# A half block's PSUM banks, the last row scatters, and the place of one expert's weight sums in a fused attention and mixture-of-experts kernel

## Chip, cores and metric

The kernel runs on one core of a Trainium2 chip. The metric is the device time of one execution in microseconds (us); lower is better. The engines are TensorE (PE, with its weight loads PEld), VectorE (DVE), ScalarE (ACT), GpSimd (POOL) and SyncE (SP, which here issues most DMAs).

## The reference

A gated linear attention is followed by a router and eight experts. Everything is float32.

```python
# q, k, v, alpha: (4, 8, 768, 48)
for t in range(S):
    state = alpha[:, :, t, :, None] * state + k[:, :, t] (outer) v[:, :, t]
    y[:, :, t] = q[:, :, t] @ state
x = y.transpose(0, 2, 1, 3).reshape(3072, 384)
...
logits = normalised(x) @ normalised(expert_emb).T / tau      # 8 experts
expert = argmax(logits); gate = softmax(logits)[expert]
out[rows of e] = gate * (relu(x[rows of e] @ w1[e]) @ w2[e])  # w1 384x1024, w2 1024x384
```

A token goes to one expert only, so its row of the output is one scaled product of that expert's two layers.

## The kernel before, in words

**Attention and routing.** The 3072 tokens are 24 chunks of 128 (NS = 24). A loop over s runs NS + 3 turns as a software pipeline: a chunk's decays are made in turn s, its scores in s + 1, its state and output in s + 2, its row of logits (`rows`) behind that. `scores` (L559) makes the products of keys and queries in two halves; the first half is masked by DVE (L571), the second is copied by ACT (L572) and masked by POOL with an `affine_select` (L573). From time to time a group of chunks is routed: `place` counts where each token belongs, and `to_rows` (L312) scatters the rows of a chunk with an indirect DMA issued by POOL (L313) to `xs`, a buffer in DRAM sorted by expert. Chunks wait for this in the list `send`. In turn s < NS one or two chunks are sent; from s = NS on all that are left. `behind(s)` puts an instruction after the last ones of turn s; `tc.issue_after` does the same with one named instruction. Both set only the order on an engine and the place in the program.

**Experts.** They are taken in an order found at run time, each with its turn i from 0 to 7. `xs` is read back in blocks of 128 rows (`xg`). PE transposes a block (`pxg`, L837), DVE or ACT copies it to `xT` (L841). The first layer gives `hT`, the second `y`, which POOL scatters to the rows of `out` (L812). Turn 0 is the leading expert: two of its blocks were read early and their first layer (`phe`, `ehT`) and second layer (L901, scaled by DVE at L904, columns `esx`) are done among the last routing work. Then it has one plain block (`first_layer` L889 and L893, `second_layer` L895 to L906). Turns 1 to 7 are *pairs*: three blocks. In the first layer all three go through Strassen-like products: `first_layer_pair` (L976) multiplies sums of `w1` and `xT`, each over 192 columns of tokens, into four PSUM banks `pq0` to `pq3` (matmuls L994, DVE sums through `by_dve` L917, ACT L1002 and L1005). In the second layer block 2 is plain, and blocks 0 and 1 go through `second_layer_pair` (L1027, matmuls L1042, DVE L1049).

Three kinds of sums feed these products:

- `mix_weights` (L931): eight POOL subtractions over `w2` of one expert into `w_m` (L941, some 1 us each). `turn_of(done_pair)` places them behind what is in `done_pair`: the last product, the last DVE operation and the last scatter of the pair before. For expert 1 there is no such pair, so `done_pair` is at first the list `routed`, that is the counts of the routing and the first two scatters of pad rows.
- `mix_hidden` (L943): DVE sums of `hT` into `hT_m`, for two `f` at a time, placed by `filled` (L920) among the next first-layer products.
- `mix_first` (L971): DVE sums for the next expert's first layer.

**Half blocks.** An expert can have more rows than its full blocks hold. `run_extra` (L1148) loads the number of such half blocks of 64 rows, behind `done_pair`, and enters a run-time If (L1151, L1155). Inside, `half_block` (L1074) has two groups of 48 small matmuls (L1084; 96 in the profile's counts), each group into one bank that `bank()` hands out of `pq0` to `pq3`, with a relu by ACT (L1089). Then come 32 in the second layer (L1097), DVE scales one half of the result (L1102) and ACT the other (L1103), and a POOL scatter follows (L812). On this data the If is taken in turns 0, 3 and 4. After turn 3 `run_rest` (L1168) tests once whether any expert has more.

**PSUM.** Pool `ps_q` has the banks `pq0` to `pq3`, one buffer each; `ps_y` has the bank `pyo`, two buffers in turn, for the plain second layer. The scheduler places instructions by these dependences, and a product of the next expert goes ahead of the If where the banks and order allow it.

The functions that the diff touches follow.

Of the kernel before, what the change touches and what calls it, by code (L numbers as in the profile page):

```python
# [9 lines left out]
FP32 = mybir.dt.float32  # L10
# [17 lines left out]
def kernel(  # L28
# [12 lines left out]
    nc = tc.nc  # L41
    B, H, S, D = q.shape
    E, DM = expert_emb.shape
    F = w1.shape[2]
    P = 128
# [4 lines left out]
    NS = N // P  # L50
# [149 lines left out]
    with ExitStack() as c1:  # L200
# [258 lines left out]
        def behind(s):  # L459

            queue = ExitStack()
            for call in st[s]["last"]:
                queue.enter_context(tc.issue_after(call.ins))
            return queue
# [94 lines left out]
        def scores(s):  # L559

            d = st[s]
            kr, qs = d["kr"], d["qs"]
            d["sm"] = sm = [work.tile([P, NP, P], FP32, name=f"sm{hh}") for hh in range(2)]
            sc = [ps_sc.tile([P, NP, P], FP32, name=f"sc{hh}") for hh in range(2)]
            for p in range(NP):
                for hh in range(2):
                    sl = slice(DP * hh, DP * hh + DP)
                    mm(
                        sc[hh][:, p], lhsT=kr[sl, p], rhs=qs[sl, p], start=True, stop=True
                    )  # L570
            nc.vector.tensor_tensor(sm[0], sc[0], causal.to_broadcast([P, NP, P]), ALU.mult)  # L571
            nc.scalar.copy(sm[1], sc[1])  # L572
            nc.gpsimd.affine_select(  # L573
                out=sm[1], in_=sm[1], pattern=[[0, NP], [1, P]], base=0,
                channel_multiplier=-1, compare_op=ALU.is_ge, fill=0.0,
            )
# [106 lines left out]
        for s in range(NS + 3):  # L683
            if s + 2 <= NS:
                v_last = load(s + 2)
            if s + 2 == NS:

                with tc.issue_after(v_last.ins):
                    weights(0)
            if 0 <= s - 1 < NS:  # L690
                with in_turn():
                    keys_back(s - 1)
            if s < NS:
                decays(s)
            if s == NS:
                with in_turn():
                    turn_early()
            if s < NS:
                decay_queries(s)
            if 0 <= s - 1 < NS:  # L700
                decay_state(s - 1)

                with in_turn(), tc.issue_after(st[s]["a_scan"].ins) if s < NS else ExitStack():
                    scores(s - 1)
            if s == 0:
                with behind(s), in_turn():
                    prepare_first(a0)
                with behind(s):
                    prepare_logits()
            if NS <= s < NS + 2:  # L710
                with in_turn():
                    first_layer_early(2 * (s - NS), 2 * (s - NS) + 1)
            if 0 <= s - 2 < NS:
                with in_turn():
                    mix_states(s - 2)
                with in_turn():
                    mix_chunk(s - 2)
            if 0 <= s - 1 < NS:

                with in_turn(), tc.issue_after(st[s]["a_scan"].ins) if s < NS else ExitStack():  # L720
                    update(s - 1)
            if 0 < s < NS and s % NCH == 0:

                with in_turn():
                    keys_back(s, ps_mm, "mm")
            if NS <= s < NS + 2:
                with in_turn():
                    first_layer_early(2 * (s - NS) + 1, 2 * (s - NS) + 2)
            if 0 <= s - 2 < NS:
                with in_turn():  # L730
                    rows(s - 2)
            if s == 1:
                with in_turn():
                    turn_logits()
            if s == 2:
                with behind(s):
                    routing_constants()
            if s == 3:
                with behind(s):
                    convert_constants()  # L740
            if 4 <= s < 4 + NXG * (NC + 1):
                i, t = divmod(s - 4, NC + 1)
                with behind(s):
                    nc.gpsimd.memset(xg_s[i][:, t], 0.0)
            if s == 3:
                with behind(s):
                    nc.gpsimd.memset(blank, 0.0)

            for g in placed_at.get(s, ()):
                r = GROUPS[g][1] - 1  # L750
                with in_turn():
                    n = place(g, r in (S0 - 1, NS - 1))
                if r == S0 - 1:
                    with behind(s):
                        first_expert(n)
            with behind(s) if s < NS else ExitStack():
                for c in send[:] if s >= NS else send[: 1 + (len(send) > 2)]:
                    to_rows(dest[:, c : c + 1], x_g[group_of[c]][:, c - GROUPS[group_of[c]][0]])
                    send.remove(c)
                    if c == S0 - 1:  # L760
                        fetch_early()
            if s == NS - 1:
                weights(1)
            r = s - 2
            if 0 <= r < NS:
                g = group_of[r]
                if r == GROUPS[g][1] - 1:
                    choose(g)
                    with behind(s) if s < NS else ExitStack():
                        nc.gpsimd.tensor_copy(x_g[g][:, :, TK], toks[:, slice(*GROUPS[g])])  # L770
            if s > NS:
                with in_turn():
                    first_layer_early(2 * (s - NS) + 2, 2 * (s - NS) + 4)
# [6 lines left out]
    with ExitStack() as c3:  # L780
# [24 lines left out]
        def bank(j=None):  # L805
            if j is None:
                taken.append(0)
                j = len(taken) % 4
            return ps_q.tile([P, 512], FP32, name=f"pq{j}")
# [85 lines left out]
        def second_layer(w2_t, hT, gate, col):  # L895

            py = ps_y.tile([P, DM], FP32, name="pyo")
            y = yp.tile([P, DM], FP32, name="y")
            with pe_turn():
                for f in range(FT):  # L900
                    pe[:] = [nc.tensor.matmul(  # L901
                        py, lhsT=hT[:, f], rhs=w2_t[:, f], start=(f == 0), stop=(f == FT - 1),
                    )]
            nc.vector.tensor_scalar(y, py, gate, None, ALU.mult)  # L904
            with turn_of(drained):
                return scatter(y, col)  # L906
# [167 lines left out]
        def half_block(w1_t, w2_t, xT, gate, col):  # L1074

            hT = hp.tile([P, FT, HALF], FP32, name="hT_half", bufs=1)
            for f0 in range(0, FT, 4):
                ph = bank()[:, 0 : 4 * HALF]

                for f in range(4):  # L1080
                    for k in range(KT):
                        for i in range(2):
                            c0 = (f0 + f) * P + i * HALF
                            nc.tensor.matmul(  # L1084
                                ph[i * HALF : (i + 1) * HALF, f * HALF : (f + 1) * HALF],
                                lhsT=w1_t[:, k, c0 : c0 + HALF], rhs=xT[:, k],
                                start=(k == 0), stop=(k == KT - 1), skip_group_check=True,
                            )
                nc.scalar.activation(  # L1089
                    hT[:, f0 : f0 + 4].rearrange("p f t -> p (f t)"), ph, AF.Relu  # L1090
                )

            py = ps_y.tile([P, DM], FP32, name="pyo")[:, 0 : DM // 2]
            y = yp.tile([P, DM], FP32, name="y")
            for f in range(FT):
                for i in range(2):
                    nc.tensor.matmul(  # L1097
                        py[i * HALF : (i + 1) * HALF], lhsT=hT[:, f],
                        rhs=w2_t[:, f, i * DM // 2 : (i + 1) * DM // 2],
                        start=(f == 0), stop=(f == FT - 1), skip_group_check=True,  # L1100
                    )
            nc.vector.tensor_scalar(y[0:HALF, 0 : DM // 2], py[0:HALF], gate, None, ALU.mult)  # L1102
            nc.scalar.mul(y[0:HALF, DM // 2 :], py[HALF:], gate)  # L1103
            scatter(y[0:HALF], col)

        def run(i):
# [32 lines left out]
                    drained.append(nc.gpsimd.drain())  # L1139
            gate, col = gt_s[i % NG], sx_s[i % NG]  # L1140
            for t in range(2 if pair else 0, blocks_run(i)):
                second_layer(
                    w2_t, hT[:, :, t * P : (t + 1) * P], gate[:, t : t + 1], col[:, t : t + 1]
                )
            if pair:
                second_layer_pair(w2_t, hT, gate, col)

# [109 lines left out]
```

## Time and profile before

| what | value |
|---|---|
| median of 3 runs | 427.87 us (427.85 to 428.65) |
| profiled execution, its own time | 429.66 us |
| its span | 427.9 us |
| instructions in the span | 10636 |
| granted clock of TensorE, mean | 1.00 |
| PE busy | 412.1 us (96%) |
| VectorE busy | 276.6 us (65%) |
| ScalarE busy | 177.3 us (41%) |
| GpSimd busy | 191.7 us (45%) |

The profile shows one execution. The span runs from the first to the last instruction; the execution's own time has 1.8 us more. A timeline row has the start (from the span's start) and the duration in us, the engine, the line of the code, the operation with its tiles, how often it ran in a row, and in brackets the idle time of that engine ahead of it and what ended it. The last routing work lies from about 144 to 163 us, the early blocks and the first layer of turn 0 from 163.6 to 182.6, turn 0's plain second layer and half block from 182.6 to 193.5. After that a pair starts at about every 31 us, and the ones behind a half block 6 us later.

### The profile page before, as it was taken

How to read it: one execution, taken by the hardware profiler on the slowest of the kernel's cores; microseconds unless marked ns; L12 is line 12 of the kernel's file. 1: busy time of each engine (PE TensorE's matmuls, PEld its weight loads, DVE VectorE, ACT ScalarE, POOL GpSimd, SP SyncE). 2: the span in 40 equal slices, each digit the busy share in tenths (PEclk: the TensorE clock that was granted, in tenths of full speed). 3: DMA queues.
4: the chain of work that ended last, by engine and by line, in shares of the span. 5: the costliest groups of instructions: out<-in, count | busy, mean ns of one | idle time of the engine just before them, and what ended most of it. 6: DMA issues, size and time to landing. Idle time of an engine off the chain costs nothing. (4 is left out here: it accounts for less than half of the span.)

```text
span 427.9 us, 10636 instructions
## 1 busy us (share of the span) xinstructions
PE 412.1 (96%) x3962; PEld 363.6 (85%) x3962; DVE 276.6 (65%) x725; ACT 177.3 (41%) x430; POOL 191.7 (45%) x283
## 2 busy tenths in 40 slices
PE   7999999999999999999999999999999999998995
PEld 6988889888898876779799799798888979978984
DVE  6888778788798424945856846823781684683631
ACT  4455454554455435363623523522361352352410
POOL 6455776677865628801018027024501802702601
PEclk9999999999999999999999999999999999999999
DMA  8999899999979903859009119016502801001001
GB/s 138 158 155 165 145 205 184 195 184 201 197 170 333 351 36 120 276 196 373 6 17 343 57 46 361 5 54 209 163 20 89 303 2 36 20 1 52 1 17 38
DMA packets 119371, 60.15 MB, mean 141 GB/s; under 512 B 102287, under 2 KB 113816, under 8 KB 119312
## 3 DMA queue, kind: packets, MB, share of 16 engines
q1 hardware_dynamic: 115208, 49.14, 49.2%
q0 software_dynamic: 3728, 10.16, 6.7%
q8 instruction: 38, 0.62, 0.7%
q14 instruction: 21, 0.17, 0.1%
q10 hardware_dynamic: 376, 0.05, 0.1%
HBM read 49.69 MB, written 11.45 MB: 143 GB/s over the span
## 5 line engine op out<-in xcount | busy, mean ns | idle before, releaser
L812 POOL DMA_INDIRECT out_dram<-y,sx x25 | 24.5, 979 | 164.5 <-DVE xT_m L971 81.1
L994 PE MATMUL pq<-xT,w 128*128 128x192 f32 x280 | 64.3, 328 | 1.0 <-PEq L1155 0.6
L994 PEld LDWEIGHTS pq<-xT,w 128*128 128x128 f32 x280 | 47.4, 190 | 2.5 <-issue 2.5
L917 DVE TENSOR_TENSOR hT<-pq,v 128x192 f32<-128x192 f32 x84 | 29.9, 356 | 27.9 <-PE pq L994 25.6
L507 POOL TENSOR_TENSOR qs<-qc,a 128x512 f32<-128x512 f32 x24 | 30.7, 1278 | 37.0 <-DVE a L503 22.6
L901 PE MATMUL pyo<-w,hT 128*128 128x384 f32 x128 | 43.3, 492 | 0.0
L994 PE MATMUL pq<-xT_m,w_m 128*128 128x192 f32 x168 | 36.8, 328 | 2.7 <-ACTq L1155 1.2
L901 PEld LDWEIGHTS pyo<-w,hT 128*128 128x128 f32 x128 | 23.7, 190 | 15.3
L1002 ACT ACTIVATE hT<-hT 128x384 f32<-128x384 f32 (+1 forms) x56 | 24.7, 443 | 24.4 <-DVE hT L917 19.5
L479 DVE TENSOR_TENSOR_SCAN r<-pa,inr 128x511 f32<-128x511 f32 x24 | 29.2, 1218 | 7.6 <-PE pa L194 7.1
L994 PEld LDWEIGHTS pq<-xT_m,w_m 128*128 128x128 f32 x168 | 28.7, 190 | 3.7 <-ACTq L1155 1.8
L503 DVE TENSOR_TENSOR_SCAN a<-pa,ini 128x512 f32<-128x512 f32 x24 | 29.3, 1223 | 1.1
L1042 PE MATMUL pq<-w_m,hT_m 128*128 128x192 f32 x168 | 29.6, 326 | 0.0
L941 POOL TENSOR_TENSOR w_m<-w 128x384 f32<-128x384 f32 x28 | 27.6, 1005 | 4.0 <-DMA out_dram<-y,sx 1.7
L1002 ACT ACTIVATE hT<-pq 128x192 f32<-128x192 f32 x28 | 9.3, 331 | 47.3 <-PE pq L994 47.3
L917 DVE TENSOR_TENSOR v<-pq,v 128x192 f32<-128x192 f32 x56 | 20.0, 357 | 13.7 <-PE pq L994 6.0
L191 PE MATMUL sc<-qs,kr 64*128 64x128 f32 x384 | 28.6, 290 | 0.0
L313 POOL DMA_INDIRECT xs<-x,dest x24 | 24.4, 1016 | 9.4 <-issue 4.5
L1042 PEld LDWEIGHTS pq<-w_m,hT_m 128*128 128x128 f32 x168 | 27.7, 190 | 0.0
L191 PEld LDWEIGHTS sc<-qs,kr 64*128 64x128 f32 x384 | 24.1, 193 | 4.2 <-issue 3.0
L941 POOL TENSOR_TENSOR w_m<-w,w_m 128x384 f32<-128x384 f32 x28 | 27.0, 998 | 0.0
L191 PE MATMUL pyx<-sm,vt 128*64 128x128 f32 x384 | 26.3, 279 | 0.0
(199 smaller groups left out, 896.1 us busy)
## 6 DMA issues: line engine op xcount, KB each, us to landing
w<-in_moe_w_dram SPq DMA_DIRECT2D x16, 1536.0 KB
kt<-in_k_dram SPq DMA_DIRECT2D x24, 192.0 KB
qt<-in_q_dram SPq DMA_DIRECT2D x24, 192.0 KB
vt<-in_v_dram SPq DMA_DIRECT2D x24, 192.0 KB
xg<-xs SPq DMA_DIRECT2D x22, 196.5 KB
at<-in_alpha_dram SPq DMA_DIRECT2D x24, 168.0 KB
xg<-xs SPq DMA_DIRECT2D x8, 98.2 KB
at<-in_alpha_dram SPq DMA_DIRECT2D x24, 22.5 KB
```

The lines of the kernel that those rows point to most:

```text
L191: last["pe"] = nc.tensor.matmul(*args, **kwargs)
L313: ins = nc.gpsimd.indirect_dma_start(out=xs, out_offset=bass.IndirectOffsetOnAxis(ap=rows, axis=0), in_=x, in_offset=None, bounds_check=E ...
L479: nc.vector.tensor_tensor_scan(r[:, L - 2 :: -1], pa[:, L - 1 : 0 : -1], inr[:, L - 2 :: -1], 1.0, ALU.mult, ALU.add,)
L503: d["a_scan"] = by_dve = nc.vector.tensor_tensor_scan(a, pa, ini, 0.0, ALU.mult, ALU.add)
L507: by_pool = nc.gpsimd.tensor_tensor(qs.rearrange("p n t -> p (n t)"), d["qc"], a, ALU.mult)
L812: ins = nc.gpsimd.indirect_dma_start(out=out, out_offset=bass.IndirectOffsetOnAxis(ap=col, axis=0), in_=y, in_offset=None, bounds_check=N - 1,
L901: pe[:] = [nc.tensor.matmul(py, lhsT=hT[:, f], rhs=w2_t[:, f], start=(f == 0), stop=(f == FT - 1),)]
L917: dve[:] = [call(*args)]
L941: nc.gpsimd.tensor_tensor(to[:, f], x[:, f], y[:, f], ALU.subtract)
L994: pe[:] = [nc.tensor.matmul(to, lhsT=left, rhs=right, start=start, stop=stop, skip_group_check=True,)]
L1002: return nc.scalar.activation(h, p, AF.Relu)
L1042: pe[:] = [nc.tensor.matmul(to, lhsT=left[:, f], rhs=right[:, f], start=start and f == 0, stop=stop and f == n - 1, skip_group_check=True,)]
```

## The change

There are three edits.

1. `scores` keeps the mask instruction, `d["masked"]`. In turn NS - 1 no chunk is sent; from turn NS on all that are left are sent, and their scatters are placed behind the mask of the last chunk.
2. The half block's first layer writes to `pyo` of `ps_y`, where before it asked `bank()` for one of the pair's banks.
3. `run` keeps the scatter that the leading expert's plain block issues, and appends it to `done_pair`. `mix_weights` of expert 1, and `run_extra` of turn 0, stand behind it.

```diff
-            nc.gpsimd.affine_select(
+            d["masked"] = nc.gpsimd.affine_select(
                 out=sm[1], in_=sm[1], pattern=[[0, NP], [1, P]], base=0,
...
-            with behind(s) if s < NS else ExitStack():
-                for c in send[:] if s >= NS else send[: 1 + (len(send) > 2)]:
+
+            with behind(s) if s < NS else tc.issue_after(st[NS - 1]["masked"].ins):
+                n_now = len(send) if s >= NS else 0 if s == NS - 1 else 1 + (len(send) > 2)
+                for c in send[:n_now]:
                     to_rows(dest[:, c : c + 1], x_g[group_of[c]][:, c - GROUPS[group_of[c]][0]])
...
             for f0 in range(0, FT, 4):
-                ph = bank()[:, 0 : 4 * HALF]
+                ph = ps_y.tile([P, DM], FP32, name="pyo")[:, 0 : 4 * HALF]
...
             for t in range(2 if pair else 0, blocks_run(i)):
-                second_layer(
+                sent = second_layer(
                     w2_t, hT[:, :, t * P : (t + 1) * P], gate[:, t : t + 1], col[:, t : t + 1]
                 )
+            if not pair:
+
+                done_pair.append(sent)
             if pair:
                 second_layer_pair(w2_t, hT, gate, col)
```

In the built program of the changed kernel, POOL's order at the start of the experts is six pad scatters in a row, the scatters of the two early blocks and of the plain block, the load of the number of half blocks, the half block's scatter, and then the eight sums for expert 1. On PE, the first three products of the next expert stand ahead of the If at turns 0, 1, 2, 4, 5 and 6, and one at turn 3.

## The prediction

> **What bounds the kernel now.** I read the page's busy shares first, then a table by stage, then the idle times of PE in the timeline, then the VectorE (DVE) and GpSimd (POOL) rows beside them.
>
> ```profile
> span 427.9 us, 10636 instructions
> ...
> PE 412.1 (96%) x3962; PEld 363.6 (85%) x3962; DVE 276.6 (65%) x725; ACT 177.3 (41%) x430; POOL 191.7 (45%) x283
> ```
>
> PE is the bound: it idles for some 15 us in all. The change adds and removes no matmul, so it can only gain idle time of PE, and the terms below are stretches of it. The granted clock is 1.00 in nearly every stage, so durations can be carried over as they stand. The timeline of PE has the idle times that the change can touch (start, duration, group, and in brackets the idle time before it with what ended it):
>
> ```profile
> 180.43 0.55 PE L837 MATMUL pxg<-ident,xg 128*128 128x128 f32 x3 [0.82 <-DVE xT L841]
> ...
> 255.53 0.92 PE L994 MATMUL pq<-xT_m,w_m 128*128 128x192 f32 x4 [0.62 <-ACTq L1155]
> ...
> 286.06 3.34 PE L1084 MATMUL pq<-xT,w 128*64 128x64 f32 x96 [0.51 <-DVE y L1049]
> ...
> 304.94 0.92 PE L994 MATMUL pq<-xT,w_m 128*128 128x192 f32 x4 [0.76 <-DVE hT L917]
> ...
> 325.06 3.25 PE L1084 MATMUL pq<-xT,w 128*64 128x64 f32 x95 [0.51 <-DVE y L1049]
> ...
> 362.20 0.92 PE L994 MATMUL pq<-xT_m,w_m 128*128 128x192 f32 x4 [0.62 <-ACTq L1155]
> ...
> 394.17 0.81 PE L994 MATMUL pq<-xT_m,w_m 128*128 128x192 f32 x4 [0.98 <-issue]
> ```
>
> They are of four kinds: a late copy of xT; half blocks (turns 3 and 4) that wait for a bank of the pair (0.51 twice); waits around the run-time If (L1155); and one wait for DVE in expert 4. The first and the last have one cause, on DVE:
>
> ```profile
> 171.33 5.12 DVE L859 TENSOR_TENSOR xg<-xg,used 128x2 f32<-128x2 f32 x1
> ...
> 203.06 0.42 DVE L917 TENSOR_TENSOR hT_m<-hT 128x256 f32<-128x256 f32 x1
> ...
> 302.75 1.87 DVE L917 TENSOR_TENSOR hT_m<-hT 128x256 f32<-128x256 f32 x1
> ```
>
> An operation on two columns takes 5.12 us, and the same kind of hT_m sum takes 0.42 in expert 1 and 1.87 in expert 4. Beside them in time stand w2 sums of POOL:
>
> ```profile
> 168.76 1.97 POOL L941 TENSOR_TENSOR w_m<-w 128x384 f32<-128x384 f32 x2
> 170.68 3.84 POOL L941 TENSOR_TENSOR w_m<-w,w_m 128x384 f32<-128x384 f32 x4
> 174.49 1.94 POOL L941 TENSOR_TENSOR w_m<-w 128x384 f32<-128x384 f32 x2
> ...
> 194.75 0.92 POOL L812 DMA_INDIRECT out_dram<-y,sx  x1 [12.91 <-ACT y L1103]
> ...
> 302.39 1.94 POOL L941 TENSOR_TENSOR w_m<-w 128x384 f32<-128x384 f32 x2
> ```
>
> The reader is to see that the DVE operation ends when the chain of eight sums does: 171.33 + 5.12 = 176.45 beside 174.49 + 1.94 = 176.43, and 302.75 + 1.87 = 304.62 beside 304.33. So a DVE sum of two SBUF tensors that starts inside such a chain (7.7 us) is held to its end plus up to 0.28. In expert 4 the hold is 1.87 - 0.42 = 1.45 us and PE idles 0.76; so PE has 0.69 us of slack there. Where the hold is less (0.16 in expert 5, 0.53 in 6, 0.44 in 7) no idle time of PE follows. I use "hold less 0.69" as the price.
>
> One rule speaks against this reading. The Trainium skill (SBUF — State Buffer, "SBUF: two separate sides") says that the shared port pair goes to whoever starts first for the whole of one instruction. By that a DVE sum would wait for about one POOL sum (1 us), and no chain could hold it for five. The 5.12 us row spans five POOL sums, so the measurement decides; the rule is the first rival's ground.
>
> **Part 1, last scatters behind the last mask.** Four POOL scatters of about 1 us (L313, 144.64 to 149.53) now follow the last mask (149.54 to 150.19 before). The mask comes some 4 us earlier. What it feeds starts at 153.9, so 3.7 us of slack already cover it, and PE there waits on other work: 0.63 us at 150.86, for ACT's ycols. The scatters end 0.65 later; the copy of toks (152.48) could slip by 0.2, and what needs its result starts at 157.2. Bounds: a gain of 0.63 (that whole idle time), a loss of 0.2. I take 0, the slack being the nearer row.
>
> **Part 2, half block in the plain second layer's banks.** The built order of the two kernels shows a second effect. Since the half block no longer uses the pair's four banks, the first three products (six matmuls, 0.98 us) of the next expert go ahead of the half block's If at every turn but 3, where one product (0.33) does. Only turns 0, 3 and 4 take the half block. Gains: the two waits of 0.51, and the stretched groups of 96 matmuls, 3.34 - 3.02 = 0.32 at turn 3 and 3.25 - 3.02 = 0.23 at turn 4 (3.02 is the group at 187.94, that had no such wait). At turns 2 and 5 the wait for ACT's branch (0.62) becomes the bare branch of PE, 0.30 in turn 1: gain 0.32 each. At turn 6 the idle 0.98 lies inside work that now precedes the If; bounds 0 and 0.98.
>
> What is late next is the POOL chain. It waits for the half block's scatter where there is one, and starts 2.4 us after its last matmul starts. Before, the first hT_m sum started 9.57 us after the next expert's first product (193.49 and 203.06). With products ahead of the If, the half block and the chain come 0.98 later, and the first sum does not: the hold grows by that. In PE's terms the place where it waits is pinned to the end of the chain, so gains after the half block are given back:
> - Turn 3: +0.51 + 0.32 - 0.33 (the product moved ahead) = **+0.50**; expert 4 stays pinned, and its 0.76 grows by what is saved after the half block.
> - Turn 4: +0.51 + 0.23, and the 0.29 before the next first product; the hold becomes 0.16 + 0.98 + 0.29 = 1.43, idle 0.74: **+0.29**.
> - Turn 5 (no half block; the chain stays where it is): +0.32, hold 0.53 + 0.32 = 0.85, idle 0.16: **+0.16**.
> - Turn 2: hold 0.31 + 0.32 = 0.63, under 0.69: **+0.32**.
> - Turn 6: if all of 0.98 is gained, hold 0.44 + 0.98 = 1.42, idle 0.73: **+0.25**.
> - The half block's second bank must first be read by the plain block's DVE scaling, which takes 0.6 us and has the 3 us of the first group (at turn 0), or the pair's whole second layer, to be done in. Nothing is taken for it, but 0.1 at each of two half blocks for a wait that may come up: **-0.20**.
>
> **Part 3, expert 1's sums behind expert 0's rows.** The eight sums leave 168.76 to 176.43. Then L859 costs about 0.15 instead of 5.12, the copies of xT are in time, and the 0.82 at 180.43 goes: **+0.82**. DVE has two-input operations beside POOL's scatters (L971 at 178.63, two in 1.28, beside scatters at 177.90 and 179.19), so scatters do not hold them. In the built order the sums come behind the half block's scatter of expert 0: 194.75 + 0.98 + 0.92 = 196.65, and end at 204.32, release 204.60. The first hT_m sum of expert 1 would have ended at 203.06 + 0.42 = 203.48: hold 1.12, idle **-0.43**. Behind this sum on DVE stand the sums that free the pair's banks; that is how PE is reached. The sums themselves are first needed at 214.72, 10 us later. SP's queue is not moved.
>
> **Sum.** 0.82 - 0.43 + 0.32 + 0.50 + 0.29 + 0.16 + 0.25 - 0.20 = 1.7 us. The profiled execution took 429.66 with a span of 427.9 (1.8 around it): 428.0 with a span of 426.2. That execution is 1.8 above the median; the same gain from the median 427.87 gives **426.2**.
>
> **The rivals.**
> - *POOL lets DVE in between two sums.* In expert 2 a hT_m sum beside the chain took only 0.68, so it can happen; the 5.12 and 1.87 rows speak against. Then nothing is pinned: 0.82 + 0.32 + (0.51 + 0.32 + 0.76 + 0.48 at turn 3) + (0.51 + 0.23 + 0.29) + 0.32 + 0.98 - 0.20 = 5.3, so 422.6. Chance 0.08.
> - *The change does little.* The idle time before xT stays, because another DVE operation stands before the copy (L971 sums of 0.65 each lie there), and the code after turn 6's jump is late in any place. Then 0.82 and 0.25 are missing: 0.6 gained, 427.2. If the half block meets another wait of the 0.51 kind for its new bank, 427.9. The waits are this small, so some of them may reappear. Chance 0.26.
> - *Slower: expert 1's sums start later than reckoned.* They wait for the half block's scatter and the list of counts. In expert 4 the chain started at 296.65, 2.5 us behind the end of the half block's scatter at 294.09, since a pad scatter waited ahead of it; at turn 0 pads for expert 3 could do the same. From the hold on, each us later is one us of PE: 1.7 is used up at +1.7, and slower by over 0.2% begins at 2.6. At +2.5, as in expert 4, 428.7; at +3.5, 429.7. In the built order the pad scatters come ahead of the half block, which speaks against it. Chance 0.07.
>
> **How the numbers follow.** About 0.2% (0.86 us) is what a measurement of this kernel can tell from no change: faster is below 427.01, slower above 428.73. The forecast (425.0 to 427.0) has 0.59. Faster is forecast and first rival, 0.67; same, the second, 0.26; slower 0.07. The range runs from 424.2 (the forecast with turn 6's whole 0.98, the ycols 0.63 and a turn 0 without a hold, rounded up by one more small term) to 427.9, which takes in the second rival and leaves out 0.15.
>
> **What would show it.** Right: L859 at 0.15; no 0.82 at the xT turn; the half blocks' groups at 3.0 with no DVE wait; expert 1's L941 rows from about 196 to 204, its first hT_m row some 1.5 long with 0.4 of PE idle after it; the same in expert 5; about 1.2 to 1.7 of idle in expert 4. Wrong: hT_m rows of 0.6 to 0.9 in all experts (first rival), a new wait at the half blocks (second), or L941 of expert 1 from 198 on (third).

## The result and the profile after

The forecast was wrong. The changed kernel took 428.89 us (428.54 to 430.28, 4 runs) beside 428.01 for the kernel before, ratio 1.0024 with a 95% interval of 0.9999 to 1.0049. A second measurement (e5 below) gave 427.18 beside 426.25, ratio 1.0014, 1.0003 to 1.0025. The medians are 0.9 us apart both times (the ratios stand for 1.0 and 0.6 us, and the first interval just reaches to no change), where 1.7 us less were forecast.

The page of the changed kernel, two of its lines:

```profile
span 428.2 us, 10643 instructions
...
PE 414.1 (97%) x3962; PEld 365.2 (85%) x3962; DVE 274.4 (64%) x725; ACT 178.1 (42%) x430; POOL 191.6 (45%) x283
```

The two spans can't be subtracted as they stand: the early second layer starts at 163.60 in the profile of before and at 162.68 in this one, and nothing that the change touches lies in most of that stretch. I compare from there on. A stage runs from the first row of one plain second layer to that of the next; its length is the difference of two start times. The third column is the kernel with the first edit alone (run e10, a second profile with the expert part in the order of before). The changed kernel stands there twice, from the first measurement and from the second (run e5); e6 is the run of that name below.

| stage | before | first edit alone | changed | changed, e5 | e6 | forecast of the change |
|---|---|---|---|---|---|---|
| early blocks, to turn 0's plain layer | 18.98 | 19.02 | 17.93 | 17.94 | 17.94 | -0.82 |
| turn 0 | 26.88 | 26.87 | 27.71 | 27.61 | 27.60 | +0.43 |
| turn 1 | 30.61 | 30.68 | 30.47 | 30.47 | 30.46 | 0 |
| turn 2 | 30.96 | 30.96 | 30.80 | 30.81 | 30.81 | -0.32 |
| turn 3 | 38.99 | 38.70 | 38.72 | 38.45 | 38.42 | -0.50 |
| turn 4 | 36.70 | 36.40 | 36.70 | 36.56 | 36.56 | -0.29 |
| turn 5 | 31.07 | 31.07 | 30.46 | 30.47 | 30.46 | -0.16 |
| turn 6 | 30.37 | 30.71 | 32.99 | 31.03 | 29.40 | -0.25 |
| turn 7 and end | 19.71 | 19.70 | 19.70 | 19.70 | 19.70 | 0 |

Until turn 6 the changed kernel is 1.40 us ahead of before (the forecast without the 0.20 kept for small waits: 1.66). Turn 6 then loses 2.62 in the first measurement. In the second it loses 0.66 beside before and 0.32 beside the first edit alone. The waits of PE in the changed kernel, here and below in its first measurement (total, times, longest):

```profile
PE pq L996 <- PEq L1160: 2.6, 1, 2.6
PE pq L996 <- DVE hT L919: 2.3, 3, 1.4
```

Neither the wait for xT nor the two for DVE's y at the half blocks is in that list any more. The first line is new: it is one wait, at turn 6's If. PE's timeline there:

```profile
389.84 0.49 PE L996 MATMUL pq<-xT,w 128*128 128x192 f32 x2
390.16 0.81 PE L996 MATMUL pq<-xT_m,w_m 128*128 128x192 f32 x4
393.61 0.98 PE L996 MATMUL pq<-xT,w 128*128 128x192 f32 x2 [2.63 <-PEq L1160]
394.38 0.85 PE L996 MATMUL pq<-xT_m,w_m 128*128 128x192 f32 x2
395.02 1.49 PE L996 MATMUL pq<-xT,w 128*128 128x192 f32 x4
```

The reader is to see two things. The three products ahead of the If (six matmuls) stand where the built order put them, and then PE idles 2.63 us: in the trace the branch of PE's sequencer takes 3.82 us there, where turn 5's takes 0.34. And behind the wait four matmuls take 1.49 us instead of 0.81. The table by stretches, whose column ahead of the DMA share is the granted clock, says why (0.84 as a mean; between 393.2 and 396.5 us it is 0.50):

```profile
389.00:400.00 11.00, 8.37 (x43) 8.11 (x42) 3.44 (x10) 1.75 (x5) 8.76 (x10) 0.84 0.11 39
```

The number that the branch tests had been loaded by 389.52 us, 0.1 ahead of the branch. What PE does wait for is seen in the DMA table: between 384 and 389.6 us it has no row for instructions at all, and between 389.6 and 393.5 it has this one:

```profile
q8 instruction: 1, 0.02, 2.2%
```

That transfer of 16 KB starts at 390.62, 1.0 us after the branch began, and takes 1.40; 1.42 later the branch ends. The same 1.3 to 1.4 us lie between the two ends in e1, e3, e4 and e5. So PE fetched the code behind the If only when it jumped there. A transfer behind a jump is not by itself a wait: at turn 5 one starts at 360.33, 1.2 us after the branch began, and the branch is over in 0.34. The 0.98 us of before at turn 6 is the same wait, two matmuls later: a transfer starts there at 391.73 and takes 1.02, and the next matmul, at 394.17, comes 1.42 after its end. The Trainium skill (Runtime: NRT & Kernel Launch, "Instruction fetch mechanics") says that a taken branch to a target outside the pages at hand forces a fetch before execution goes on; the trace agrees, and gives it a price.

The other reading of the prediction holds. DVE's operation on two columns (L859 of before), the first hT_m sums of experts 1 and 4 behind it, then expert 1's chain and the end of expert 4's on POOL, and PE's waits for these sums:

```profile
173.09 0.15 DVE L861 TENSOR_TENSOR xg<-xg,used 128x2 f32<-128x2 f32 x1
...
201.21 1.57 DVE L919 TENSOR_TENSOR hT_m<-hT 128x256 f32<-128x256 f32 x1
...
300.41 2.49 DVE L919 TENSOR_TENSOR hT_m<-hT 128x256 f32<-128x256 f32 x1
```

```profile
194.80 1.96 POOL L943 TENSOR_TENSOR w_m<-w 128x384 f32<-128x384 f32 x2
196.71 3.87 POOL L943 TENSOR_TENSOR w_m<-w,w_m 128x384 f32<-128x384 f32 x4
200.54 1.95 POOL L943 TENSOR_TENSOR w_m<-w 128x384 f32<-128x384 f32 x2
...
300.67 1.94 POOL L943 TENSOR_TENSOR w_m<-w 128x384 f32<-128x384 f32 x2
```

```profile
202.15 0.49 PE L996 MATMUL pq<-xT,w 128*128 128x192 f32 x2
203.10 0.92 PE L996 MATMUL pq<-xT,w_m 128*128 128x192 f32 x4 [0.46 <-DVE hT L919]
203.85 0.49 PE L839 MATMUL pxg<-ident,xg 128*128 128x128 f32 x3
...
303.22 0.92 PE L996 MATMUL pq<-xT,w_m 128*128 128x192 f32 x4 [1.38 <-DVE hT L919]
```

Chain and sum end together again (202.49 and 202.78; 302.61 and 302.90). The holds are 1.15 and 2.07 us, PE's idle times 0.46 and 1.38: both are the hold less 0.69.

### The profile page after: what moved, and what is told of

Same layout as the page of the kernel before. It is cut to its first block, busy times and chain, and to the rows that moved or that the text cites. A ratio compares the mean times of both kernels' runs of the same rounds, so it can differ in the third digit from the quotient of the medians.

```text
span 428.2 us, 10643 instructions
## 1 busy us (share of the span) xinstructions
PE 414.1 (97%) x3962; PEld 365.2 (85%) x3962; DVE 274.4 (64%) x725; ACT 178.1 (42%) x430; POOL 191.6 (45%) x283
## 5 line engine op out<-in xcount | busy, mean ns | idle before, releaser
L996 PE MATMUL pq<-xT,w 128*128 128x192 f32 x280 | 65.6, 333 | 3.2 <-PEq L1160 2.6
L1051 DVE SCALAR_TENSOR_TENSOR y<-pq,gt,u 128x192 f32<-128x192 f32 x21 | 8.8, 418 | 26.5 <-PE pq L1044 26.5
```

Of the source, the lines that this page charges most:

```text
L996: pe[:] = [nc.tensor.matmul(to, lhsT=left, rhs=right, start=start, stop=stop, skip_group_check=True,)]
```

## The experiments

**Theory A**: turn 6's long branch comes from the place of the If in PE's code. **Theory B**: the products ahead of the If make it long. **Theory C**: the earlier gain wasn't there. Each run has the kernel before measured beside it, and the ratios are to that: its median was 426.13 us for e1 to e4, 426.25 for e5 to e8 and 426.44 for e9 to e12. The expectations of e1 to e3 reckon from the 428 of the first measurement, so their times are some 2 us too high. The code can be moved without adding anything that runs: `run_rest` holds a loop that this data never enters, and every matmul in it adds 4 instructions to PE's code ahead of turn 4. This edit, with again = 6 or 2, is the one of e1, e2 and e3 (the loop's second layer is begun early and started anew, so it would compute the same):

```diff
-            for f in range(FT):
+            for f in [*range(again), *range(FT)]:
                 for i in range(2):
                     nc.tensor.matmul(
                         py[i * HALF : (i + 1) * HALF], lhsT=hT[:, f],
...
-                        half_block(w1_t, w2_t, xT, gate[0:HALF], col[0:HALF])
+                        half_block(w1_t, w2_t, xT, gate[0:HALF], col[0:HALF], 6)
```

**e1, the changed kernel, code of turns 4 to 7 moved by 48 instructions.**

> The changed kernel with 12 more matmuls in a loop of run_rest that this data never enters (the second layer of its half block is begun 12 matmuls early and started again): nothing that runs is added, but the code of turns 4 to 7 stands 48 PE instructions later. Theory A (the 2.63 us of idle PE at turn 6's If come from where that If stands in PE's code): turn 6 shows an If like turn 5's, no idle of over 0.4 us there and no stretch at half the clock behind it; expert 7's first hT_m sum is then held by the chain for 1.0 to 1.5 us as in expert 5 (0.3 to 0.8 us of PE idle); time about 2.6 us below the changed kernel, 425.5 to 426.6. Theory B (the products moved ahead of the If make the branch late): turn 6 keeps its 2.6 us, time 428.5 to 429. Theory C (the gain of the earlier turns was not there): turn 6 may go, but expert 6 ends less than 1 us earlier than before, time 427.0 to 428.

425.48 us beside 426.13, ratio 0.9974 (0.9961 to 0.9987). Turn 6's branch takes 0.41 us and PE has no idle time there. But the same edit made the jump over the loop 48 instructions longer, and now that branch takes 3.73 us and PE idles at turn 3:

```profile
290.52 0.89 PE L996 MATMUL pq<-xT_m,w_m 128*128 128x192 f32 x4 [2.93 <-PEq L1173]
```

So the long branch went from one jump to another with the place of the code, and no instruction that runs had changed. B falls for turn 6. The number agrees with A's (425.5 to 426.6) only by chance: A's range stood for 1.4 to 2.5 us below the kernel before, and 0.65 was measured by the medians (1.1 by the ratio), since the new stall at turn 3, which was not foreseen, took the rest.

**e2, the kernel before, moved by 16**, to within one instruction of where the changed kernel has turn 6's If.

> The kernel before, with 4 such matmuls in the same loop that is never entered: turns 4 to 7 stand 16 PE instructions later, which puts turn 6's If within one instruction of where it stands in the changed kernel. Its order on all engines is that of before, no product is ahead of turn 6's If. Theory A: the 0.98 us of turn 6 become some 3 us of idle PE with a slow stretch behind, expert 7's first hT_m sum is no longer held; time 430 to 431.5. Theory B: no change, 427.8 to 428.2.

425.09 us, ratio 0.9984 (0.9970 to 0.9997). A's number was missed: the branch took 0.67 us, and the 0.98 of idle time that before has at turn 6 was gone (29.40 us for that stage). The DMA table has one instruction row between 382 and 386.7, ahead of this branch, where the changed kernel has none; the branch ends 1.40 us after that transfer does. So whether the code is there in time decides, and the place alone does not settle that at one instruction's distance. What else does, stays open, and B is not refuted here.

**e3, the kernel before, moved by 48.**

> The kernel before with the 12 matmuls that are never run: turn 6's If stands 48 instructions later. Theory A: the 0.98 us of idle PE behind turn 6's If go, but expert 7's first hT_m sum is then held longer by the chain (0.44 + 0.98 = 1.4 us), and PE idles about 0.7 us for it: 427.4 to 428.0, 0 to 0.4 below before. If the 0.98 belongs to anything but the place of the code, it stays.

427.16 us, ratio 1.0021 (1.0008 to 1.0035). Turn 6 lost its 0.98 and took 29.40 us instead of 30.37; turn 3's jump over the loop took 3.38 us and PE idled 2.7 us, as in e1. A's number was missed, as that stall was not foreseen here either, and the 0.7 us that expert 7 was to wait did not come. Without any product ahead of an If the kernel before can be made to have the same stall. That is the second blow for B.

**e4, as e1, with the first hT_m sums later.**

```diff
-                    if f % 2 == 1:
-                        fill.extend(mix_hidden(hT, f - 1, f + 1))
+                    if f >= 2:
+                        fill.extend(mix_hidden(hT, 2 * f - 4, 2 * f - 2))
```

> The changed kernel moved by 12 as in the first run, and the first four hT_m sums of a pair are placed among the products of f = 3 instead of f = 2, so that they start 3 us later, behind the end of the chain of w2 sums. If the hold of DVE by that chain is what keeps PE waiting (0.46, 1.38, 0.45 us in experts 1, 4, 5, and about 0.5 expected in expert 7), these waits go and nothing takes their place: 2 to 2.8 us below the first run, 423 to 424.3. If the waits come from something else in f = 2, they stay and the time is that of the first run. A cost may be that eight sums instead of four stand in f = 3 and behind it, and the pair's second layer waits for hT_m (up to 0.5 us each).

423.15 us, ratio 0.9927 (0.9915 to 0.9940): 2.3 us below e1, with e1's stall at turn 3 still in it. No wait for hT is left in the list of PE's waits.

**e5, the changed kernel again.**

> The changed kernel once more, beside the runs below. Theory A (the place of turn 6's If in PE's code): its branch takes near 3.8 us again and PE idles 2.6 us, time 0 to 1.5 us above the kernel before, as in the first measurement. If the long branch comes and goes from execution to execution, the times of single runs lie in two groups some 3 us apart.

427.18 us, ratio 1.0014 (1.0003 to 1.0025). The branch took 3.18 us and PE idled 2.13, in a profile whose clock stayed at 1.00:

```profile
386.00:400.00 14.00, 11.87 (x73) 11.60 (x72) 6.32 (x18) 3.52 (x10) 9.67 (x10) 1.00 0.09 30
```

The stall is in both profiles of the changed kernel; what differs is the clock behind it. Four of the 12 executions took 425.4 to 425.9 us at a mean clock of 0.999 or more, the profiled one among them; eight took 426.9 to 427.8 at 0.995 or less. So the four are below the kernel before (426.25), stall and all, and the eight some 1.7 us longer. In e3, which has the stall at turn 3, it is the same: four at 425.5 to 426.3 with 0.999, eight at 427.1 to 429.0 with 0.995 or less. In the kernel before, executions at 0.993 and at 1.000 take the same time (425.87 and 426.18, for instance), so it matters where the clock falls. That it falls behind the stall is seen in the first profile above; of the eight no profile was kept.

**e6, the changed kernel moved by 16** (again = 2).

> The changed kernel with 4 matmuls in the loop that is never entered (16 instructions, where the first run had 48): turn 6's If is moved away, and the jump over that loop at turn 3 is 16 instructions longer and not 48, so that it should stay as short as in the changed kernel (0.43 us; 3.73 in the first run). Theory A: neither turn 3 nor turn 6 has a branch of over 0.7 us; the sum of the prediction holds: 1.2 to 2.2 us below the kernel before, with waits for hT of about 0.46, 1.4, 0.45 and 0.3 to 0.8 us in experts 1, 4, 5, 7. Theory B (the products ahead of the If make the branch late): turn 6 keeps 2.6 us, time as the run above.

423.82 us, ratio 0.9942 (0.9929 to 0.9955): 2.4 us below before and 3.4 below e5. Turn 3's branch takes 0.43 us, turn 6's 0.41, and PE's list of waits has hT with 2.1 us in three waits:

```profile
PE pq L996 <- DVE hT L919: 2.1, 3, 1.2
```

PE's timeline at turn 6 beside that of the changed kernel above:

```profile
387.02 0.49 PE L996 MATMUL pq<-xT,w 128*128 128x192 f32 x2
387.34 0.81 PE L996 MATMUL pq<-xT_m,w_m 128*128 128x192 f32 x4
388.30 0.56 PE L996 MATMUL pq<-xT,w 128*128 128x192 f32 x2
```

The same instructions follow each other at once. A holds, B and C fall: this is what the change does without the late code, a little more than forecast (1.7), with the forecast holds in experts 1, 4 and 5. Expert 7's did not come as expected: its first hT_m sum took 1.19 us (from 396.21) and was through 0.85 before the chain ended (398.25), and no wait for it is in PE's list.

**e7, e6 with the later hT_m sums of e4.**

> The run above with the first four hT_m sums of a pair among the products of f = 3 instead of f = 2. If the hold of DVE by the chain of w2 sums sets PE's waits in experts 1, 4, 5 and 7, they go: 2.2 to 3 us below the run above, 3.5 to 5 below the kernel before. If the branch at turn 6 is long again in this build (its code is moved 6 instructions further by the other order), 3 us of that are lost.

420.11 us, ratio 0.9853 (0.9839 to 0.9868): 3.7 us below e6, more than expected, and the fastest kernel of the study. All waits for hT are gone. From plain layer to plain layer turn 0 takes 26.72 us (27.60 in e6), turn 3 37.32 (38.42), turn 4 35.83 (36.56). Turns 2 and 6 gain 0.34 and 0.35 too. There e6's list names no wait, but four matmuls start some 0.24 us late after a hold of 0.76 and 0.77 (at 262.13 and 397.72).

**e8, the third edit alone.**

> The third edit alone on the kernel before (the w2 sums of expert 1 behind expert 0's rows). By the prediction: L859 takes 0.15 us instead of 5.12 and the 0.82 us of idle PE ahead of the last block's transposes go; the chain of expert 1 starts behind the half block, about 1 us earlier than in the whole change since no product is ahead of the If, so that expert 1's first hT_m sum is held 0.1 to 0.4 us and PE does not wait: 0.7 to 1.1 us below the kernel before. Rival: the saved time is lost again before expert 1's second layer, 0 to 0.2 below.

425.04 us, ratio 0.9973 (0.9962 to 0.9983): 1.2 below, just over what was expected. The early stage takes 17.93 us. Expert 1's first hT_m sum takes 0.94, a hold of 0.52 (0.1 to 0.4 expected), and PE does not wait, as the price of "hold less 0.69" has it.

**e9, the second edit alone, moved by 16.**

> The second edit alone (half block in pyo), with the 4 matmuls that are never run, which keep turns 3 and 6 clear of long branches in the run of the whole change. The chain of expert 1 stays where it was before, so the 0.82 us ahead of the early transposes and L859's 5.12 us stay, and expert 1's first hT_m sum is not held. Turns 1 to 6 should gain what they gain in that run: 0.15 + 0.15 + 0.57 + 0.14 + 0.61 + 0.97 = 2.6 us below the kernel before, bounds 1.6 to 2.9. If the third edit were needed for these gains, less than 1.

425.19 us, ratio 0.9984 (0.9962 to 1.0006), which is no clear answer: the 12 executions go from 424.32 to 429.21, and in the profiled one the attention, which the edit does not touch, took 1.5 us longer than in the first edit's. The stages from the early blocks on are 1.76 us shorter than there: turn 5 by 0.61, turn 6 by 1.29, but turn 0 longer by 0.61 without any hold. The 2.6 expected had counted nothing for that. The rows show where it is lost, behind the half block:

```profile
193.49 0.49 PE L994 MATMUL pq<-xT_m,w_m 128*128 128x192 f32 x2
194.11 0.92 PE L994 MATMUL pq<-xT,w 128*128 128x192 f32 x4
194.97 0.59 PE L994 MATMUL pq<-xT_m,w 128*128 128x192 f32 x2
```

Two matmuls start 0.62 us before the next (0.33 elsewhere), and four 0.86 (0.65 elsewhere): 0.5 us in small waits. PE's rows name no releaser, but those of its weight loads (PEld) do: they idle 0.43 us ahead of 194.11 for ACT's copy `v` (L1005), and 0.23 ahead of 194.96 for DVE's sum `v` (L917). Both read a bank of a product that went ahead of the half block. In this build two products stand ahead of turn 0's If. In the changed kernel three do, and its rows behind turn 0's half block show no such wait.

**e10, the first edit alone.**

> The first edit alone (last four row scatters behind the last mask). Prediction: no change, bounds 0.63 us below the kernel before (the wait for ycols gone) and 0.2 above it. The mask should end some 4 us earlier and the scatters 0.65 us later; the stretch from the first early first-layer product to the early second layer should last as long as before.

426.45 us, ratio 0.9999 (0.9990 to 1.0008). No change, as forecast. The last mask starts ahead of the four scatters, and the early stage takes 19.02 us (18.98 before). The shifts were not those that were forecast: POOL waits for ACT ahead of the mask,

```profile
144.14 0.64 POOL L573 TENSOR_SCALAR_AFFINE_SELECT sm<-sm 128x512 f32<-128x512 f32 x1 [1.92 <-ACT sm L572]
```

so that, counted from POOL's operation ahead of it (L532, at 141.60; 143.88 before), the mask comes 3.1 us earlier and the scatters end 2.6 later, not 4 and 0.65. The slack was enough for that.

**e11, the kernel before with the later hT_m sums.**

> The kernel before with the first four hT_m sums of a pair among the products of f = 3. If the chain holds DVE there as read, only expert 4's 0.76 us of idle PE can go, since in the other experts the hold stays under 0.69 us: 0.5 to 1.0 below the kernel before. On top of the whole change the same move was worth 3.7 us. If it is worth near 3 us here too, the move helps by something else than the hold, and the whole change had lost nothing to the chain. Turn 6's If stands 6 instructions later than before, which may move that turn by up to 1 us either way; the stage of expert 4 is read by itself.

425.18 us, ratio 0.9968 (0.9956 to 0.9979): 1.3 us below before, against 3.7 on top of the change (e6 to e7). In the profile the stage of turn 3 is 1.03 us shorter than in e10. So by these two, some 2.4 of the 3.7 us had first been lost to the chain by the change itself. Turn 6 did move: in the profiled execution (427.00, the longest of seven; the others took 424.96 to 425.44) PE idled 2.31 us behind its jump, and then ran at half speed for a few us (four matmuls in 1.48). The others were not profiled, so whether they have the stall is not known.

**e12, e7 with 2 matmuls in place of 4.**

> The fastest version so far (the change, the later hT_m sums, and matmuls that are never run) with 2 of these matmuls in place of 4, so that turn 3's landing behind the loop and turn 6's If stand 8 instructions earlier. In the version with 4, PE idled 0.58 us some 3 us behind the jump at turn 3, waiting for nothing that the profile shows. By theory A this is code too and moves or goes: 0 to 0.6 us below that version, 419.5 to 420.2; if turn 6 becomes long, 422 to 423.5.

420.75 us, ratio 0.9862 (0.9845 to 0.9879): no better than e7 and above what was expected. The 0.58 us of idle PE behind turn 3's jump are gone (turn 3 takes 36.79 us instead of 37.32), as A had it, but the attention of the profiled execution took 1 us longer, and the two ratios can't be told apart.

## Why the prediction was wrong

The step that failed is turn 6: "bounds 0 and 0.98", and +0.25 taken. It measured 2.62 us the other way in the first measurement (2.28 by the first edit's run) and 0.32 to 0.66 in the second. The prediction had seen that the 0.98 us of idle time ended with no releaser, and its second rival said that "the code after turn 6's jump is late in any place"; but it bounded a loss at nothing. Two things came in its place. The wait for code grew: PE idled 2.63 and 2.13 us where it had idled 0.98. And in the first profile the clock fell to 0.50 for 3.4 us behind it, where the prediction had carried all durations over at 1.00. By the two groups of e5 the late code alone leaves the changed kernel below before, and the slow clock, some 1.7 us, puts it above.

In the built program the change moves the If by 17 instructions of PE's code, from a place where the code gave out two matmuls behind the jump (394.17 above) to one where the branch itself waits. e1 and e6 show that the place of code is the cause: instructions that never run take the stall away. They give no rule for the place: in e2, moved by 16, the branch waited 0.3 us and not 3.4. The row of before that could have warned is the very one that was quoted. Where the code is not late (e6), turn 6 gained 0.97 and not 0.25, since the hold that was to give 0.73 back was 0.77 and not 1.42.

That the sum until turn 6 comes out near (1.40 for 1.66) is in part luck, as its terms are off by up to 0.45 both ways.

Point by point, with the table of stages:

- **Third edit.** Right: L859's 5.12 us became 0.15, and the 0.82 of idle time went. The stage gained 1.05, since the idle time in a row is counted from the modelled end of the matmul before it; from start to start each such wait costs 0.2 to 0.3 us more.
- **Expert 1's hold.** Right in mechanism and size (1.12 and 0.43 forecast, 1.15 and 0.46 measured). Turn 0 still lost 0.83, because the wait costs more than its 0.46: in the rows above, 0.95 us lie between the starts of 202.15 and 203.10 where 0.33 is usual, and 0.75 behind that where 0.65 is, which makes 0.72. Without the hold (e7) turn 0 takes 26.72, less than before.
- **The 0.20 for small waits.** Mis-sized: nothing at turn 0, and 0.5 at turn 3, where one product alone stands ahead of the If. There the weight loads wait 0.43 us (at 292.26) for ACT's copy `v` and 0.24 (at 293.12) for DVE's sum `v`, as in e9.
- **Turn 3.** Half of the 0.50 (0.27). The stretched groups of matmuls (0.32, and 0.23 at turn 4) were nothing that the change removes: both profiles of the first measurement have them (3.34 and 3.25 before, 3.31 and 3.18 changed), and none of e5, e6 and e10 (3.02 each). In e2, e8 and e10 turn 3 is 0.3 us shorter with the order of before. One profile was read as if it always ran so. In these later runs turn 3 gained 0.25 (e5) and 0.28 (e6) against e10. Expert 4's idle time went from 0.76 to 1.38, as forecast (1.2 to 1.7).
- **Turn 4.** Nothing instead of 0.29, and 0.16 lost in e5 and e6 against e10. The 0.23 of the stretch was not there to gain; expert 5's hold was 1.14, and PE idled 0.45, which again costs more from start to start.
- **Turns 1, 2 and 5.** 0.14, 0.16 and 0.61 gained for 0, 0.32 and 0.16. At turn 5 the hold that was forecast did not come: expert 6's sum, in the middle of the chain, got in between two sums of POOL:

```profile
369.23 0.51 DVE L919 TENSOR_TENSOR hT_m<-hT 128x256 f32<-128x256 f32 x1
```

- **The rule on the port** (the Trainium skill, SBUF — State Buffer, "SBUF: two separate sides"), by which the pair is held for one whole instruction, fits this row and expert 2, where DVE waits for one POOL instruction at most. It does not explain expert 4's 2.49 us, which outlast two. Which of them happens stays open.
- **First edit.** Nothing, as forecast (e10), though the mask and the scatters moved by other amounts than read.
- **The slower rival** named a cause that was not there: expert 1's chain started at 194.80, 0.02 behind the half block's scatter. The second rival's 427.9 is 427.8 by its own terms.

## What to carry to other kernels

Idle time of PE behind a run-time branch that nothing releases was code being fetched here. Instructions added or moved ahead of it turned 1 us into 2 to 3 (the changed kernel, e11) or into 0 (e2, e3), so such a term is to be bounded on both sides, and judged with the code moved a little both ways. What the clock does behind a long wait belongs to the bound. When a stall is removed ahead of a chain on another engine, look for the place that is pinned to the end of that chain: here the chain took back about half of the gain until the DVE sums were placed behind its end (e6 is 2.4 us below before and e7 6.1, of which 1.3 can be had without the change, e11). And a stretch in one profile is a term of a sum only if a second run has it too.

## What the runs showed of the hardware

A jump over code that was not at hand cost PE's branch 3.2 to 3.8 us instead of 0.3 to 0.4 (changed kernel, e1, e3, e4, e5), made of 0.8 to 1.0 us until the 16 KB transfer starts, 0.9 to 1.4 for it, and 1.3 to 1.4 from its end until the branch ends. After such an idle time of 2.1 to 2.9 us PE ran on at full clock in some executions (e1, e3 and e5 in their profiles) and at half speed for a few us in others: 0.84 over 11 us in the changed kernel, in e11 (four matmuls in 1.48 us), and in e4

```profile
291.19 1.49 PE L996 MATMUL pq<-xT,w 128*128 128x192 f32 x4
```

for four matmuls that take 0.81 elsewhere. What decides it was not tried.
